# Order of the Gram and value products, and of the rounding steps of the hidden activations, in an attention and SwiGLU kernel

## The chip, the cores and the metric

The kernel runs on one core of one Trainium2 chip. The metric is the device time of one execution in microseconds (us); lower is better. Three runs of the kernel before took 283.43, 283.50 and 283.79 us, a median of 283.5.

## The reference

A polynomial-sketch attention is followed by a SwiGLU feed-forward block. `S1` and `S2` are 8 x 32 sketches.

```python
# q, k, v: (4 batches, 4 heads, 1088 tokens, 32)
def phi(x):                       # 64 features a token
    a = einsum('rd,bhsd->bhsr', S1, x); b = einsum('rd,bhsd->bhsr', S2, x)
    return einsum('bhsi,bhsj->bhsij', a, b).reshape(..., 64)
kv  = einsum('bhsf,bhsd->bhfd', phi(k), v);  z = phi(k).sum(2)
att = einsum('bhsf,bhfd->bhsd', phi(q), kv) / (einsum('bhsf,bhf->bhs', phi(q), z) + 1e-6)
x   = att, rearranged to (4352 tokens, 128)
g = x @ w_gate                    # 128 x 1536
out = (g * sigmoid(g) * (x @ w_val)) @ w_out    # w_out: 1536 x 128
```

The denominator needs only the sums of the key features. Since a feature is a product of two sketches, these sums are the 8 x 8 matrix of inner products of the two key sketches over the tokens: the "Gram" product of the code.

## The kernel before, in words

**Tokens and units.** The 4352 tokens are worked on transposed: 128 model dimensions on the partitions, tokens along the free axis. They are split into blocks: three of 384, 320 and 384 tokens for batch 0, then blocks of 480 and a last one of 384. The 1536 hidden columns are 12 chunks of 128. One block and one chunk make a *unit*: a gate product, a value product, a silu of the gate, a multiplication to the hidden activation `h`, and later a *down* product of `h` with `w_out` (`down`, L1024 or the cut form L1017, L1019, L1020).

**Cut products.** From the late units of the third block on, the gate and value products use operands that are cut into a rounded part, a remainder and a difference, so that they run in a shorter matmul format. For a unit, `start_unit` issues two products with the difference `xd` into a pair of PSUM banks (L937) and a scaling of that pair on ScalarE (L940). `finish_unit` issues four more products into the same banks (L949, L950), the silu on ScalarE (L952) and the multiplication on VectorE (L957). Three pairs of banks go around; the multiplication frees a unit's pair for the unit after the next two.

**The hidden activations.** For most chunks of the later blocks the down product is cut as well (the list `DOWN`). `cut_hidden` prepares three operands from `h`: the rounded `h1` (on ScalarE at L913, for some chunks on VectorE at L911), the remainder `h0 = h - h1` on GpSimd (L914), and `hd` on VectorE (L917), a difference of the scaled `h1` and `h`. It does not issue them at once. It puts them into two dictionaries by the number `y` of a unit: what is in `before` is issued inside `finish_unit(y)` ahead of the four products and the silu, what is in `behind` after the multiplication. The cut down product comes some five units later.

**Attention beside it.** Batch 0's attention is written out ahead. For batches 1 to 3 the generator `attentions` issues one step each time it is advanced (`parts_of`, `group`), between the units of the feed-forward block. A batch goes through: transposes of keys and queries, sketches of keys by matmul (`key_products`, L354) with copies on ScalarE (L566), features on VectorE (`key_features`, L377), the Gram product `gram` (L589) with a copy to SBUF on ScalarE (L595), the products of features and values `key_values` (L388), all into one bank, then `fold`: a small product (L601) that turns the Gram sums by the transposed sketch, and a multiplication on VectorE (L602) that leaves the denominators' weights in `s123`. `spread_out` turns and spreads the values' sums (L687 and six DMAs on SyncE) and loads the next batch's values. After that come the query sketches with `s123` (`query_sketches`, L342), the query features (`query_step`) and the numerators (L740), whose copies are the next tokens of the feed-forward block.

`turn_sketch` makes the transposed sketch once: a copy `four` on ScalarE (L578), a transposing product (L579) and a copy (L582).

**Order.** Nothing is scheduled by a tool: each engine runs its instructions in the order in which the program issues them, and waits on semaphores where data or buffers need it. So the order of the calls is the order of every engine's queue.

Of the kernel before, what the change touches and what calls it, by code (L numbers as in the profile page):

```python
# [12 lines left out]
AF = mybir.ActivationFunctionType  # L13
# [6 lines left out]
def kernel(  # L20
# [28 lines left out]
    nc = tc.nc  # L49
    P = nc.NUM_PARTITIONS  # L50
# [6 lines left out]
    NC = (NX + 3) // 4  # L57
    F = R * R
# [38 lines left out]
    def touch(*which):  # L97
        for i in which:
            clock[0] += 1
            used[i] = clock[0]  # L100
# [11 lines left out]
    def bank(tag=None):  # L112

        if tag is not None:
            i = place[tag]
        else:
            i = place[free_banks[turn[0] % len(free_banks)]]
            turn[0] += 1
        touch(i)
        return PS[:, i, :]  # L120

    def pair(keep=None):

        i = min((i for i in (0, 4, 6) if i not in held), key=lambda i: max(used[i], used[i + 1]))
        touch(i, i + 1)
        if keep is not None:
            held.add(i)
            kept[keep] = i
        return PS[:, i : i + 2, :]
# [3 lines left out]
    def let_go(keep):  # L133
        i = kept.pop(keep)
        held.discard(i)
        touch(i, i + 1)
# [26 lines left out]
    def load_k(b):  # L163
        nc.sync.dma_start(
            out=kld[:, 0:NX, :], in_=k[b].rearrange("h (pp x) d -> (h pp) x d", pp=32)
        )
# [158 lines left out]
    def turn_k(c0, c1):  # L325
        four = "p (a c) d -> p a c d"
        nc.vector.transpose(
            out=kT[:, c0:c1, :, :].rearrange("p c a t -> p a c t"),
            in_=kld[:].rearrange(four, a=4)[:, :, c0:c1, :],
        )  # L330
# [53 lines left out]
    def key_values(kv, phk, c0, c1, order=range(NC)):  # L384

        for c in range(c0, c1):
            for h in range(H):
                nc.tensor.matmul(  # L388
                    kv[32 * h : 32 * h + 32, 0:F],
                    vld[:, h, c, :],  # L390
                    phk[:, c, h, :, :].rearrange("p i j -> p (i j)"),
                    start=(c == order[0]),
                    stop=(c == order[-1]),
                )
# [148 lines left out]
    def turn_keys(b):  # L543

        for c in kpieces:
            turn_k(*c)
            if c[1] == NC and b + 1 < B:
                load_k(b + 1)
            yield
# [22 lines left out]

    sketch_turned = const.tile([P, P], FP32, name="s1t")

    def turn_sketch(ps):

        four = apool.tile([P, 4, H, R], FP32, tag="fold", name="four")
        nc.scalar.copy(four[:], s12[:, :, 0, :].unsqueeze(1).to_broadcast([P, 4, H, R]))  # L578
        nc.tensor.matmul(  # L579
            ps, four[:].rearrange("p a h r -> p (a h r)"), ident[:], start=True, stop=True  # L580
        )
        nc.scalar.copy(sketch_turned[:], ps)  # L582

    def gram(kv, kab):

        flat = "p x r -> p (x r)"
        for c in range(NC):
            x, a = slice(H * c, H * c + H), c % 4
            nc.tensor.matmul(  # L589
                kv[32 * a : 32 * a + 32, F : F + H * R],  # L590
                kab[:, 0, x, :].rearrange(flat), kab[:, 1, x, :].rearrange(flat),
                start=(c < 4), stop=(c >= NC - 4),
            )
        g = apool.tile([P, H * R], FP32, tag="gram", name="gram")
        nc.scalar.copy(g[:], kv[:, F : F + H * R])  # L595
        return g

    def fold(kv, g):

        ps = kv[:, 2 * F : 2 * F + H * R]  # L600
        nc.tensor.matmul(ps, sketch_turned[:], g[:], start=True, stop=True)  # L601
        nc.vector.tensor_tensor(  # L602
            out=s123[:, :, 2, :].rearrange("p (x h) r -> p x h r", x=2),
            in0=ps.rearrange("p (x h r) -> p x h r", x=1, r=R).to_broadcast([P, 2, H, R]),
            in1=own[:].unsqueeze(1).unsqueeze(3).to_broadcast([P, 2, H, R]),
            op=ALU.mult,
        )

    def attentions():

        yield from turn_keys(1)
        kp = pair("keys")
        turn_sketch(kp[:, 1, 320 : 320 + P])
        kab, copies = sketched(kp, key_products, 2, "kab2")
        run_copies(copies, 2)
        let_go("keys")
        yield from turn_queries(1)
        phk = apool.tile([P, NC, H, R, R], FP32, tag="phk", name="phk")  # L620
        yield from features(phk, kab)
        yield from turn_keys(2)
        kvz = pair("values")
        g = gram(kvz[:, 0, :], kab)
        key_values(kvz[:, 0, 0:F], phk, 0, NC)
        kab, copies = sketched(pair(), key_products, 2, "kab2")
        run_copies(copies, 2)
        fold(kvz[:, 0, :], g)
        spread = spread_out(1, kvz[:, 0, :])
        let_go("values")  # L630
        yield
        qab, copies = sketched(pair(), query_sketches, 3, "qab")
        run_copies(copies, 2)
        yield
        yield from query_step(1, qab)
        numerators(1, spread)
        yield "first"

        phk = apool.tile([P, NC, H, R, R], FP32, tag="phk", name="phk")
        yield from features(phk, kab)  # L640
        yield from turn_keys(3)
        yield from turn_queries(2)
        for b in (2, 3):
            yield "pe"
            if b == 3:
                numerators(2, spread)
            kv = bank("g2")
            g = gram(kv, kab)
            key_values(kv[:, 0:F], phk, 0, NC)
            if b == 2:  # L650
                kab, copies = sketched(pair(), key_products, 2, "kab2")
                run_copies(copies, 2)
            fold(kv, g)
            spread = spread_out(b, kv)
            yield
            yield "pe"
            qab, copies = sketched(pair(), query_sketches, 3, "qab")
            run_copies(copies, 2)
            yield
            if b == 2:  # L660
                yield from turn_queries(3)
                phk = feats[:].rearrange("p s (n h i j) -> p (s n) h i j", h=1, i=R, j=R)
                phk = phk.rearrange("p (c h) o i j -> p c (h o) i j", h=H)
                yield from features(phk, kab)
            yield from query_step(b, qab)
        yield "pe"
        numerators(3, spread)
        yield

    def run_copies(copies, n):  # L670
        for f, *args in copies[:n]:
            f(*args)
        del copies[:n]
# [102 lines left out]
    CUT = 1.0 - 2.0**-13  # L776
# [4 lines left out]
    def whole(ap):  # L781
        return ap.bitcast(FP32)
# [74 lines left out]
    before, behind = {}, {}  # L857

    def add_to(where, y, f):
        where.setdefault(y, []).append(f)  # L860
# [41 lines left out]
    def cut_hidden(y, i, j):  # L902

        if len(h_sets) < (5 if i < line[2] else OWN):
            h_sets.insert(0, next(h_rooms))
        n = SPLIT if i == LAST else blocks[i][1]
        h_sets.append(h_sets.pop(0))
        h1, h0, hd = h_parts[i, j] = [x[:, 0:n] for x in h_sets[-1]]
        h = hidden[i, j][:, 0:n]
        if j in ((2, 5, 8, 10) if i > line[2] else (9,)):  # L910
            add_to(before, y + 1, lambda: nc.vector.tensor_scalar(h1, h, CUT, None, op0=ALU.mult))  # L911
        else:
            add_to(behind, y + 1, lambda: nc.scalar.activation(h1, h, AF.Copy, scale=CUT))  # L913
        add_to(before, y + 2, lambda: nc.gpsimd.tensor_tensor(  # L914
            out=h0, in0=h, in1=whole(h1), op=ALU.subtract
        ))
        add_to(before, y + 3, lambda: nc.vector.scalar_tensor_tensor(  # L917
            out=hd, in0=whole(h1), scalar=WHOLE, in1=h, op0=ALU.mult, op1=ALU.subtract
        ))

# [196 lines left out]
    ps = bank("acc")  # L1117
# [23 lines left out]
    for t, c in zip(("acc", "g1", "g2"), (aside, c0, c1)):  # L1141
        ps = bank(t)
# [3 lines left out]
    n = steps[0][1]  # L1146
    pss = query_products(*steps[0], "ab")
    qbs = [query_copy(n, *ps) for ps in pss]
    phk = apool.tile([P, NC, H, R, R], FP32, tag="phk", name="phk")
# [10 lines left out]
    kvz = [apool.tile([P, P], FP32, name=x) for x in ("kvz0", "kvz1")]  # L1160
    nc.scalar.copy(zq[:], kz)
    kv = bank("acc")[:, 0:F]
# [7 lines left out]
    ps = bank("g0")  # L1170
# [8 lines left out]
    ps = bank("g1")  # L1179
# [16 lines left out]
    def parts_of(n):  # L1196

        for _ in range(n):
            if ahead[0] not in ("pe", "end"):
                ahead[0] = next(att, "end")  # L1200
# [96 lines left out]
    for n in range(ND):  # L1297
        if n == ND - 2:
            start_unit(2, 6)
        next_down()  # L1300
        parts_of(n in (0, 1, 7, 10, 11, 12))
        at(*steps_at.get(n, ()))
        if n == 9:
            catch_up(nc.vector)
# [58 lines left out]
    for y in range(END):  # L1363
# [16 lines left out]
        for k, c0, c1, tag, t0 in down_steps.get(y, ()):  # L1380
            if k == 0:
                n = c1 - c0
# [4 lines left out]
    ps = wide("a")[:, 0, 0:D]  # L1387
# [42 lines left out]
```

## Time and profile before

| quantity | value |
|---|---|
| median of three runs | 283.5 us |
| the profiled execution's own time | 283.42 us |
| its span | 281.7 us |
| granted TensorE clock, mean | 0.999 of full speed |
| TensorE matmul busy | 270.2 us, 96% of the span |
| VectorE busy | 221.1 us, 79% |
| ScalarE busy | 195.7 us, 69% |
| GpSimd busy | 98.7 us, 35% |
| waits of the value products (L388) for the copy of the Gram sums, in L388's own matmul row | 2.8 us, 3 times |

The profile is one execution, taken by the hardware's profiler. The span lies between its first and its last instruction; the execution's own time is some 1.7 us longer. PE is TensorE's matmul queue, PEld its weight loads, DVE is VectorE, ACT is ScalarE, POOL is GpSimd, SP is SyncE, which only issues DMAs here. A row of the timeline gives the start, the duration, the engine, the source line and operation, output and input, how often it runs in a row, and in brackets how long the engine was idle before it and which instruction ended that. A float32 matmul shows as two instructions. A row of the waits gives who waited for whom, the total in us, the number of times and the longest.

### The profile page before, as it was taken

To read this page: it belongs to the slowest core of one execution; us is meant where nothing else is said; L and a number is where in the kernel's file an instruction comes from. 1 tells how busy PE (TensorE), PEld (TensorE's weight loads), DVE (VectorE), ACT (ScalarE), POOL (GpSimd) and SP (SyncE) were. 2 spreads that over 40 slices of the span, in tenths; PEclk is the share of its full clock that TensorE was granted. 3 is DMA by queue.
4 is the path that set the end of the run, shared out by engine and by line. 5 is a ranking of instruction groups with operands and counts; after the bars stand their busy time and mean duration, and the time that the engine had idled before them with its cause. 6 is when DMAs were issued, how large, how long until landed. Compare 5 with 4: busy or idle time off the path is not lost.

```text
span 281.7 us, 5882 instructions
## 1 busy us (share of the span) xinstructions
PE 270.2 (96%) x2235; PEld 202.6 (72%) x2235; DVE 221.1 (79%) x376; ACT 195.7 (69%) x356; POOL 98.7 (35%) x110
## 2 busy tenths in 40 slices
PE   8899999997999989999999999799999999999995
PEld 7555566564895777767667878576888788789994
DVE  3997988798488762787627899976996996998871
ACT  3467665561586567777558999568888888887880
POOL 3315322064032010111016667433555553653430
PEclk9999999999999999999999999999999999999999
DMA  6584195222331041100200002000200200020021
GB/s 194 160 227 114 47 255 161 81 79 59 64 84 26 0 106 47 54 0 0 38 11 7 1 0 35 0 3 0 37 0 0 35 3 0 4 32 2 0 35 28
DMA packets 26139, 14.30 MB, mean 51 GB/s; under 512 B 19840, under 2 KB 24192, under 8 KB 26112
## 3 DMA queue, kind: packets, MB, share of 16 engines
q1 hardware_dynamic: 25456, 13.84, 19.8%
q8 instruction: 17, 0.28, 0.4%
q10 hardware_dynamic: 656, 0.10, 0.2%
q14 instruction: 10, 0.08, 0.1%
HBM read 11.41 MB, written 2.23 MB: 48 GB/s over the span
## 4 chain that ended last, share of the span: by engine, by line
PE 83%; DVE 9%; ACT 3%; issue 2%; DMA 1%; SPq 0%; DVEq 0%; ACTq 0%
PE PS L1024 15%; PE PS L937 13%; PE PS L949 13%; PE PS L950 13%; PE PS L973 10%; PE PS L1017 3%; PE PS L1019 3%; PE PS L1020 3%; PE PS L354 2%; PE PS L740 2%; PE PS L342 2%; PE PS L388 2%; DMA kld<-in_k_dram 1%; DVE phk L377 1%; DVE hbuf L957 1%
## 5 line engine op out<-in xcount | busy, mean ns | idle before, releaser
L940 ACT ACTIVATE PS<-PS 128x960 f32<-128x960 f32 (+1 forms) x90 | 83.3, 926 | 30.0 <-PE PS L937 29.0
L957 DVE SCALAR_TENSOR_TENSOR hbuf<-PS,sg 128x480 f32<-128x480 f32 (+1 forms) x87 | 55.0, 633 | 29.9 <-ACT sg L952 28.5
L952 ACT ACTIVATE sg<-PS 128x480 f32<-128x480 f32 (+1 forms) x90 | 49.6, 551 | 2.6 <-PE PS L950 2.2
L1024 PE MATMUL PS<-hbuf,wo 128*128 128x480 f32 (+3 forms) x122 | 50.7, 512 | 0.0
L937 PE MATMUL PS<-xd,graw 128*128 128x480 f32 (+1 forms) x69 | 36.0, 521 | 0.0
L937 PE MATMUL PS<-xd,wd 128*128 128x480 f32 (+1 forms) x90 | 34.0, 377 | 1.8 <-DVE hbuf L957 1.8
L949 PE MATMUL PS<-x,w 128*128 128x480 f32 (+1 forms) x90 | 33.4, 371 | 0.0
L950 PE MATMUL PS<-x,wb 128*128 128x480 f32 (+1 forms) x90 | 33.2, 369 | 0.0
L1024 PEld LDWEIGHTS PS<-hbuf,wo 128*128 128x128 f32 x122 | 22.8, 189 | 5.9 <-issue 0.4
L950 PE MATMUL PS<-x,graw 128*128 128x480 f32 (+1 forms) x69 | 25.5, 369 | 0.0
L937 PEld LDWEIGHTS PS<-xd,wd 128*128 128x128 f32 x90 | 17.0, 188 | 11.3 <-issue 4.5
L973 PE MATMUL PS<-xT,wg 128*128 128x384 f32 (+1 forms) x60 | 23.5, 474 | 0.1
L973 PE MATMUL PS<-xT,wv 128*128 128x384 f32 (+1 forms) x60 | 23.1, 467 | 0.3 <-DVE wv L286 0.3
L832 POOL TENSOR_TENSOR x<-xT,x 128x480 fp32r<-128x480 f32 (+1 forms) x6 | 7.2, 1195 | 40.7 <-ACT x L829 24.8
L914 POOL TENSOR_TENSOR hroom<-hbuf,hroom 128x480 fp32r<-128x480 f32 (+1 forms) x14 | 17.2, 1229 | 8.8 <-ACT hroom L913 4.3
L977 ACT ACTIVATE sg<-PS 128x384 f32<-128x384 f32 (+1 forms) x24 | 11.2, 468 | 13.0 <-PE PS L973 12.2
L949 PEld LDWEIGHTS PS<-x,w 128*128 128x128 f32 x90 | 16.9, 188 | 2.2
L950 PEld LDWEIGHTS PS<-x,wb 128*128 128x128 f32 x90 | 16.9, 188 | 2.1
L949 PE MATMUL PS<-x,graw 128*128 128x480 f32 (+1 forms) x48 | 18.0, 376 | 0.0
L937 PEld LDWEIGHTS PS<-xd,graw 128*128 128x128 f32 x69 | 13.0, 188 | 6.8 <-ACT PS L940 3.2
L973 PEld LDWEIGHTS PS<-xT,wv 128*128 128x128 f32 x60 | 11.2, 190 | 7.4 <-DVE hbuf L988 0.8
L973 PEld LDWEIGHTS PS<-xT,wg 128*128 128x128 f32 x60 | 10.9, 190 | 7.8 <-issue 1.1
(288 smaller groups left out, 567.6 us busy)
## 6 DMA issues: line engine op xcount, KB each, us to landing
kld<-in_k_dram SPq DMA_DIRECT2D x4, 544.0 KB, 4.0
vld<-in_v_dram SPq DMA_DIRECT2D x12, 144.0 KB, 4.8
qld<-in_q_dram SPq DMA_DIRECT2D x3, 544.0 KB, 4.0
raw<-in_moe_w_out_dram SPq DMA_DIRECT2D x4, 384.0 KB, 4.4
raw<-in_moe_w_gate_dram SPq DMA_DIRECT2D x3, 384.0 KB, 3.6
raw<-in_moe_w_val_dram SPq DMA_DIRECT2D x3, 384.0 KB, 3.7
out_dram<-o SPq DMA_DIRECT2D x16, 60.0 KB, 1.9
vld<-in_v_dram SPq DMA_DIRECT2D x4, 112.0 KB, 3.0
```

The source lines that it names most:

```text
L914: add_to(before, y + 2, lambda: nc.gpsimd.tensor_tensor(out=h0, in0=h, in1=whole(h1), op=ALU.subtract))
L937: nc.tensor.matmul(ps[:, k], w_parts[id(w), j // 3][2][:, j % 3, :], xd, start=True, stop=True)
L940: nc.scalar.activation(ps, ps, AF.Copy, scale=-1.0 / WHOLE)
L949: nc.tensor.matmul(ps[:, k], w1, x1, start=False, stop=False, skip_group_check=True)
L950: nc.tensor.matmul(ps[:, k], wb, x0, start=False, stop=True, skip_group_check=True)
L952: nc.scalar.activation(sg, ps[:, 0], AF.Silu, scale=WHOLE)
L957: nc.vector.scalar_tensor_tensor(out=hj[:, 0:n], in0=ps[:, 1], scalar=WHOLE, in1=sg, op0=ALU.mult, op1=ALU.mult)
L973: nc.tensor.matmul(o[:, 0:n], w[:, j, :], xT[:, t0 : t0 + n], start=True, stop=True)
L977: nc.scalar.activation(sg[:, 0:n], g[:, 0:n], AF.Silu)
L1017: nc.tensor.matmul(acc[i][:, 0:n], wd, hd, **sides)
L1019: nc.tensor.matmul(p, w1, h1, start=(j == mine[0]), stop=False)
L1024: nc.tensor.matmul(acc[i][:, 0:n], wo[:, j, :], hidden[i, j][:, 0:n], **sides)
```

## The change

It has three parts. (1) The copy `four` on ScalarE is issued at the start of `attentions`, two steps ahead of the product that reads it. (2) `key_values` is issued ahead of `gram`, and `fold` and `spread_out` come one step (one unit) later; for batch 1 this adds a step, and the list of units that advance the generator gets one more number, 8. (3) In `cut_hidden` the ScalarE rounding moves from behind the next unit's multiplication to ahead of its silu, the GpSimd subtraction from two units later to the next unit, and the VectorE difference from ahead of the multiplication three units later to behind the multiplication of the next unit. No instruction is added or removed on any engine. Lines behind the edits move by four to six numbers.

```diff
-    def turn_sketch(ps):
+    def four_sketches():
         four = apool.tile([P, 4, H, R], FP32, tag="fold", name="four")
         nc.scalar.copy(four[:], s12[:, :, 0, :].unsqueeze(1).to_broadcast([P, 4, H, R]))
+        return four
+
+    def turn_sketch(four, ps):
         nc.tensor.matmul(
...
+        four = four_sketches()
         yield from turn_keys(1)
         kp = pair("keys")
-        turn_sketch(kp[:, 1, 320 : 320 + P])
+        turn_sketch(four, kp[:, 1, 320 : 320 + P])
...
         kvz = pair("values")
+        key_values(kvz[:, 0, 0:F], phk, 0, NC)
         g = gram(kvz[:, 0, :], kab)
-        key_values(kvz[:, 0, 0:F], phk, 0, NC)
         kab, copies = sketched(pair(), key_products, 2, "kab2")
         run_copies(copies, 2)
+        yield
         fold(kvz[:, 0, :], g)
         spread = spread_out(1, kvz[:, 0, :])
...
             kv = bank("g2")
+            key_values(kv[:, 0:F], phk, 0, NC)
             g = gram(kv, kab)
-            key_values(kv[:, 0:F], phk, 0, NC)
             if b == 2:
                 kab, copies = sketched(pair(), key_products, 2, "kab2")
                 run_copies(copies, 2)
+            yield
             fold(kv, g)
             spread = spread_out(b, kv)
-            yield
             yield "pe"
...
         else:
-            add_to(behind, y + 1, lambda: nc.scalar.activation(h1, h, AF.Copy, scale=CUT))
-        add_to(before, y + 2, lambda: nc.gpsimd.tensor_tensor(
+            add_to(before, y + 1, lambda: nc.scalar.activation(h1, h, AF.Copy, scale=CUT))
+        add_to(before, y + 1, lambda: nc.gpsimd.tensor_tensor(
             out=h0, in0=h, in1=whole(h1), op=ALU.subtract
         ))
-        add_to(before, y + 3, lambda: nc.vector.scalar_tensor_tensor(
+        add_to(behind, y + 1, lambda: nc.vector.scalar_tensor_tensor(
             out=hd, in0=whole(h1), scalar=WHOLE, in1=h, op0=ALU.mult, op1=ALU.subtract
         ))
...
-        parts_of(n in (0, 1, 7, 10, 11, 12))
+        parts_of(n in (0, 1, 7, 8, 10, 11, 12))
```

## The prediction

> **What bounds the kernel now.** I read the shares by engine first, then the longest waits, then the timeline around each wait that stops TensorE.
>
> ```profile
> PE 270.2 (96%) x2235; PEld 202.6 (72%) x2235; DVE 221.1 (79%) x376; ACT 195.7 (69%) x356; POOL 98.7 (35%) x110
> PE 83%; DVE 9%; ACT 3%; issue 2%; DMA 1%; SPq 0%; DVEq 0%; ACTq 0%
> ```
>
> TensorE (PE) is busy for 96% of the 281.7 us span and carries 83% of the chain that ended last. A faster kernel can only come from the places where PE stands still. The waits name them:
>
> ```profile
> DVE hbuf L957 <- ACT sg L952: 28.5, 29, 3.2
> PE PS L388 <- ACT gram L595: 2.8, 3, 1.3
> PE PS L937 <- DVE hbuf L957: 1.8, 2, 1.1
> PEld PS L579 <- ACT four L578: 1.0, 1, 1.0
> ```
>
> The first line costs nothing by itself: VectorE (DVE) waits for ScalarE (ACT) while PE works. The other three stop PE, and the change touches all three. The timeline of PE shows them; the bracket is idle time before the instruction and who ended it:
>
> ```profile
> 52.09 0.81 PE L1024 MATMUL PS<-hbuf,wo 128*128 128x384 f32 x2
> 53.29 0.49 PE L579 MATMUL PS<-ident,four 128*128 128x128 f32 x2 [0.39 <-ACT four L578]
> ...
> 67.77 0.38 PE L589 MATMUL PS<-kab 128*32 128x32 f32 x18
> 69.41 1.21 PE L388 MATMUL PS<-phk,vld 128*32 128x64 f32 x72 [1.27 <-ACT gram L595]
> 70.55 1.27 PE L354 MATMUL PS<-s,kT 128*64 128x64 f32 x36
> ...
> 100.59 0.38 PE L589 MATMUL PS<-kab 128*32 128x32 f32 x18
> 101.88 1.21 PE L388 MATMUL PS<-phk,vld 128*32 128x64 f32 x72 [0.91 <-ACT gram L595]
> ...
> 141.40 0.38 PE L589 MATMUL PS<-kab 128*32 128x32 f32 x18
> 142.34 1.21 PE L388 MATMUL PS<-feats,vld 128*32 128x64 f32 x72 [0.57 <-ACT gram L595]
> ```
>
> The value products (L388) write another part of the bank that the copy of the Gram sums (L595) reads, and PE waits for that copy, which stands in ACT's queue behind other work. From 176 us on, the trouble is VectorE:
>
> ```profile
> 175.10 1.27 POOL L914 TENSOR_TENSOR hlate<-hbuf,hlate 128x480 fp32r<-128x480 f32 x1 [0.72 <-ACT hlate L913]
> 175.21 1.69 DVE L917 SCALAR_TENSOR_TENSOR hroom<-hroom,hbuf 128x480 fp32r<-128x480 f32 x1
> 176.81 0.65 DVE L957 SCALAR_TENSOR_TENSOR hbuf<-PS,sg 128x480 f32<-128x480 f32 x1
> 177.38 0.64 DVE L917 SCALAR_TENSOR_TENSOR hroom<-hroom,hbuf 128x480 fp32r<-128x480 f32 x1
> 177.51 0.49 PE L937 MATMUL PS<-xd,wd 128*128 128x480 f32 x1 [0.76 <-DVE hbuf L957]
> ```
>
> The same difference (L917) takes 0.64 us alone and 1.69 us when a GpSimd subtraction (L914) runs; it ends about 0.53 us after that one (176.37). PE waits for the multiplication (L957) queued behind it, since that frees the pair of banks. The second such stop is at 181.31 to 182.77.
>
> **Part 1, the copy `four`.** In the built order it moves on ACT from 52.95 to just ahead of the silu at 49.71, where ACT is idle for 1.39 us; that hides its 0.29 us (without the gap it would cost those). PE's pair of instructions at 52.09 takes 0.65 us by the chain, so it ends at 52.74 and L579 could start then instead of 53.29: 0.55 us. DVE was idle for 1.59 us before 56.57, waiting for the products behind this, so its queue moves up too. Bounds 0 and 0.55; I take 0.5, as nothing in the rows holds the products behind.
>
> **Part 2, values ahead of Gram, fold later.** The Gram product itself remains. Its 18 instructions, at the rate of L388 (72 in 70.55 − 69.41 = 1.14 us), are 0.29 us. So the three places give:
> - first: 1.64 − 0.29 = 1.35 us less a new wait. Working: L388, Gram, L354 (1.20 us) end at 67.77 + 2.63 = 70.40; three pairs of down products (0.27 us an instruction, 1.62) and the fold (0.24) bring PE to the query sketches (L342) at 72.26, before at 73.79. They read what the fold gives (L602). In the built order VectorE does the tokens' difference (L837, 0.56) ahead of it, and that waits for ACT: two key copies (0.69 from 70.5), then the rounding of tokens (0.53). So L602 ends near 72.5 and L342 starts near 72.6: gain 1.2. Bounds 0.6 (the fold's chain half a microsecond longer) and 1.5.
> - second: 101.88 − 100.59 − 0.29 = 1.0. VectorE's L602 now stands behind the multiplication of that unit (about 106.2), but L342 comes only near 107.
> - third: 142.34 − 141.40 − 0.29 = 0.65, covered the same way.
>
> Keys, queries, values and weights needed there are on chip (SP's order is unchanged). The six spreading DMAs and four value loads issue behind the fold, some 0 to 2 us later; their users come 14 us later or more (the values at 100.59, numerators at 88.52, 139.34, 188.63). The values' pair of banks is held one step longer; no paired unit starts in that time. Parts 1 and 2: 0.5 + 1.2 + 1.0 + 0.65 = 3.35 us.
>
> **Part 3, the rounding steps.** A unit takes PE 1.96 us when its down product is cut (158.29 to 160.25 between first products). 30 of the 46 roundings are on ACT (L913, 0.61 us; what follows starts 0.49 us later, 162.21 to 162.70). Ahead of the silu they delay it and the multiplication by 0.49 us. Slack: the multiplication at 201.61 ends at 202.26; the third-next unit's second product, which needs its bank, starts at 203.54, so 1.28 us become 0.79. New wait: the rounding waits for DVE's previous multiplication, and silu and the next bank scaling (L940) queue behind it. The circle silu to multiplication (160.40 − 159.79 = 0.61), multiplication 0.65, a hand-over of 0.08 (170.96 to 171.04, from ACT to GpSimd), rounding to silu 0.49 is 1.83 us, under 1.96: free while DVE is on time, but it catches up only 0.13 us a unit once late.
>
> What DVE gains: the subtraction starts when the rounding ends, the multiplication gives way 1.05 us later (0.61 from silu to multiplication, less 0.12 by which the silu starts before the rounding ends, and 0.57 to DVE's next instruction), the difference comes next, and the subtraction (1.23) is then nearly over: a wait of about 0.25 us instead of up to 1.05. From 160.40 to 182.07 VectorE is practically full; its differences there exceed 0.64 us by 1.0 + 0.46 + 1.05 + 1.04 = 3.55 us. Seven waits of 0.25 leave 1.75, so 1.8 is freed. Against it stand one more difference ahead of each multiplication (0.57) and the first delayed silu (0.49): net 0.7 off the two stops, which are 177.51 − 176.37 − 0.22 = 0.92 and 182.77 − 181.31 − 0.22 = 1.24, 2.16 us together. Bounds: 2.9 gained (both stops and the 0.7 before 190.83 vanish) and 2.5 lost (they double). I take 0.7, by the rows. In the wait for the last numerators (188.63 to 190.83) one more difference stands ahead of the releasing multiplication: 0.3 lost. From 196 us on no stop of PE is left to win, and 0.79 us of slack covers the delay: 0. The copies of sums and tokens on ACT keep their places.
>
> The Trainium skill, "SBUF — State Buffer", section "Who interferes with whom", has a rule that speaks against subtracting at once: a VectorE instruction with two SBUF inputs and a GpSimd one that reads SBUF exclude each other for a whole instruction, and issue order decides who blocks. The 1.69 against 0.64 us agrees with that. If by the rule every difference waited out a whole subtraction, the seven would pay 1.05 us each, 7.35 instead of 3.55, and the sum as an estimate would be a loss of 1.8 us, 285.2 us; by the starts in the rows they pay a quarter of it.
>
> Sum: 3.35 + 0.7 − 0.3 = 3.75 us; the profiled execution took 283.42 us, so 279.7 us. The median of the runs is 283.5, the same within 0.1.
>
> **Rivals.**
> - *All of VectorE's lateness goes* (differences never meet subtractions): 3.35 + 2.9 = 6.2, 277.2 us. For: the lengths alone and together. Against: the feature products (L377) still meet them. 0.13.
> - *The fold or another chain takes Part 2's place* (L342 waiting for L602; VectorE and GpSimd setting the pace at 56 to 66 us, where PE waits for `wo`): about 1.5 lost, 281.2 us. 0.12.
> - *VectorE's stops double*, since a late multiplication now holds the silu: 283.42 − 3.35 + 2.5 = 282.5 us. 0.08.
> - *Slower*: the circle through ACT becomes the bound. It does from the point where multiplications end more than 0.79 us late in most cut units; each rounding on ACT then costs PE time, and above 3.35/30 = 0.11 us each the gain is gone. At 0.15 us on 30 units: 283.42 − 3.35 + 4.5 = 284.6 us. Against: 1.83 is under 1.96. 0.09.
> - *Nothing moves*, PE's stops turning into others of the same size: 283.4 us. 0.03.
>
> **How the numbers follow.** The forecast has 0.55, with 278.6 to 280.9 as its own range. The range 277.2 to 282.5 leaves out the slower case, the unmoved one and about half of the two outer ones: about 0.2. Faster by over 0.2% (0.57 us, about what a measurement can tell): 0.55 + 0.13 + 0.12 + 0.08 = 0.88; same 0.03; slower 0.09.
>
> **What would show it.** Right: L388 starts within 0.1 us of the product ahead of it in all three places, and no wait of L388 for L595 or of L579 for L578 is listed; the mean of the 39 differences of 480 columns falls from 1.14 us (44.5 us in all) towards 0.9; PE's stops on L957 shrink. Wrong: a wait of L342 for L602 above 0.3 us; ACT idle ahead of L913, waiting for L957, in many units; PE stops on L937 after 196 us.

## The result: 280.1 us, and the profile after

The changed kernel takes 280.1 us (median of four runs, 279.65 to 280.17) against 283.64 us before (median of four runs); the ratio of the means is 0.986, 95% interval 0.983 to 0.990. A few executions take 1.4 to 2.1 us longer than the others of their kernel: one of these four of the kernel before (285.12 us), and below the profiled ones of two kernels in which GpSimd reads nothing (283.10 us beside a median of 281.02, 278.88 beside 277.43). Against the 283.5 us that the forecast starts from, the gain is 3.4 us. The forecast was 279.7 us. The profiled execution took 280.12 us with a span of 278.4 us, so 3.30 us less than the one before.

Behind the edits the lines have new numbers: L579 is now L583, L589 L593, L595 L599, L601 L605, L602 L606, L687 L693, L740 L746, L829 L835, L837 L843, L911 L917, L913 L919, L914 L920, L917 L923, L937 L943, L940 L946, L949 and L950 L955 and L956, L957 L963, L1024 L1030. L342, L354, L377 and L388 keep theirs.

The page's busy times and its chain by engine show TensorE's share up and VectorE's busy time down by 7.2 us, though VectorE executes as many instructions as before:

```profile
PE 270.4 (97%) x2235; PEld 202.9 (73%) x2235; DVE 213.9 (77%) x376; ACT 196.2 (70%) x356; POOL 102.4 (37%) x110
PE 88%; DVE 7%; ACT 2%; issue 2%; POOL 0%; DVEq 0%; ACTq 0%
```

In TensorE's own waits, those of L388 and L583 are gone. The multiplication still stops TensorE twice, for 1.5 us in sum after 1.8. They are not the same two stops: the first of before is gone, the second stands as it was (1.08 us idle, now at 178.75), and one came anew at 198.28:

```profile
PE PS L943 <- DVE hbuf L963: 1.5, 2, 1.1
```

TensorE's timeline at the places of Parts 1 and 2. L583 follows the down product directly, and L388 its predecessor without an idle bracket, in the first place and in the third:

```profile
52.20 0.81 PE L1030 MATMUL PS<-hbuf,wo 128*128 128x384 f32 x2
52.85 0.38 PE L583 MATMUL PS<-ident,four 128*128 128x128 f32 x2
...
66.59 0.70 PE L1030 MATMUL PS<-hbuf,wo 128*128 128x320 f32 x2
67.22 1.21 PE L388 MATMUL PS<-phk,vld 128*32 128x64 f32 x72
...
71.77 2.16 PE L342 MATMUL PS<-s,qT 128*32 128x96 f32 x72
73.86 0.44 PE L943 MATMUL PS<-xd,graw 128*128 128x384 f32 x1
...
137.61 1.20 PE L746 MATMUL PS<-phT,spread 32*32 32x288 f32 x34
138.74 1.21 PE L388 MATMUL PS<-feats,vld 128*32 128x64 f32 x72
```

Where the time went is read by setting the start of one and the same instruction in both profiles side by side. How much earlier it starts in the changed kernel:

| up to | before | after | earlier by | step | forecast |
|---|---|---|---|---|---|
| L579, now L583 | 53.29 | 52.85 | 0.44 | 0.44 (0.55 from the product ahead of it, 52.09 and 52.20) | 0.5 |
| first paired unit behind the first place | 75.41 | 73.86 | 1.55 | 1.1 | 1.2 |
| behind the second | 109.68 | 107.00 | 2.68 | 1.1 | 1.0 |
| behind the third | 149.88 | 146.32 | 3.56 | 0.9 | 0.65 |
| behind VectorE's two stops | 182.77 | 178.75 | 4.02 | +0.46 | +0.7 |
| behind the last numerators | 190.83 | 186.90 | 3.93 | −0.1 | −0.3 |
| behind 200 us | 216.80 | 213.59 | 3.21 | −0.7 | 0 |

Six steps stand near the forecast, within 0.25 us. The last one was not forecast: a new stop of TensorE. The timeline of VectorE, GpSimd and TensorE there:

```profile
193.82 0.36 DVE L917 TENSOR_SCALAR hroom<-hbuf 128x480 fp32r<-128x480 f32 x1
194.10 0.64 DVE L963 SCALAR_TENSOR_TENSOR hbuf<-PS,sg 128x480 f32<-128x480 f32 x1
194.32 1.23 POOL L920 TENSOR_TENSOR hroom<-hbuf,hroom 128x480 fp32r<-128x480 f32 x1 [1.54 <-DVE hroom L917]
194.67 1.39 DVE L923 SCALAR_TENSOR_TENSOR hroom<-hroom,hbuf 128x480 fp32r<-128x480 f32 x1
195.58 1.56 POOL L920 TENSOR_TENSOR hlate<-hbuf,hlate 128x480 fp32r<-128x480 f32 x1
195.99 1.67 DVE L843 SCALAR_TENSOR_TENSOR xd<-x,xT 128x480 fp32r<-128x480 f32 x1
197.58 0.65 DVE L963 SCALAR_TENSOR_TENSOR hbuf<-PS,sg 128x480 f32<-128x480 f32 x1
...
198.28 0.49 PE L943 MATMUL PS<-xd,wd 128*128 128x480 f32 x1 [0.42 <-DVE hbuf L963]
```

Read it from the top. VectorE rounds this chunk itself (L917), right ahead of the multiplication. That starts GpSimd's subtraction at 194.32, which runs to 195.55. The difference of the same chunk stands right behind the multiplication; it starts at 194.67, in the middle of the subtraction, and takes 1.39 us instead of 0.64. By then the next chunk's subtraction starts, and the token difference (L843) meets that one: 1.67 us. The next multiplication starts at 197.58, 3.48 us behind the last, and TensorE waits for the banks that it frees.

Over the whole kernel the differences tell which chunks this hits. I paired each rounding with its difference, in order. Of the 30 chunks rounded on ScalarE none takes over 1.3 us (mean of 0.77, the small blocks included); of the 16 rounded on VectorE, 13 take 1.30 us or more. Before, the long ones were spread over both kinds. The mean of the 39 of 480 columns is 1.02 us, where 1.14 was measured before and 0.9 expected.

### The profile page after: what moved, and what is told of

Same layout as the page of the kernel before. It is cut to its first block, busy times and chain, and to the rows that moved or that the text cites. A ratio compares the mean times of both kernels' runs of the same rounds, so it can differ in the third digit from the quotient of the medians.

```text
span 278.4 us, 5875 instructions
## 1 busy us (share of the span) xinstructions
PE 270.4 (97%) x2235; PEld 202.9 (73%) x2235; DVE 213.9 (77%) x376; ACT 196.2 (70%) x356; POOL 102.4 (37%) x110
## 4 chain that ended last, share of the span: by engine, by line
PE 88%; DVE 7%; ACT 2%; issue 2%; POOL 0%; DVEq 0%; ACTq 0%
PE PS L1030 17%; PE PS L943 14%; PE PS L955 13%; PE PS L956 13%; PE PS L979 10%; PE PS L1023 3%; PE PS L1025 3%; PE PS L1026 3%; PE PS L342 2%; PE PS L746 2%; PE PS L241 2%; PE PS L354 2%; PE PS L388 2%; DVE hbuf L963 1%; PE PS L1068 1%
## 5 line engine op out<-in xcount | busy, mean ns | idle before, releaser
L946 ACT ACTIVATE PS<-PS 128x960 f32<-128x960 f32 (+1 forms) x90 | 83.3, 926 | 26.6 <-PE PS L943 25.6
L963 DVE SCALAR_TENSOR_TENSOR hbuf<-PS,sg 128x480 f32<-128x480 f32 (+1 forms) x87 | 55.1, 634 | 39.9 <-ACT sg L958 33.1
L1030 PE MATMUL PS<-hbuf,wo 128*128 128x480 f32 (+3 forms) x122 | 50.7, 512 | 0.0
L943 PE MATMUL PS<-xd,graw 128*128 128x480 f32 (+1 forms) x69 | 35.8, 519 | 0.0
L943 PE MATMUL PS<-xd,wd 128*128 128x480 f32 (+1 forms) x90 | 34.1, 379 | 1.5 <-DVE hbuf L963 1.5
L955 PE MATMUL PS<-x,w 128*128 128x480 f32 (+1 forms) x90 | 33.4, 371 | 0.0
L956 PE MATMUL PS<-x,wb 128*128 128x480 f32 (+1 forms) x90 | 33.3, 370 | 0.0
L1030 PEld LDWEIGHTS PS<-hbuf,wo 128*128 128x128 f32 x122 | 22.8, 189 | 5.9 <-issue 0.4
L956 PE MATMUL PS<-x,graw 128*128 128x480 f32 (+1 forms) x69 | 25.5, 369 | 0.0
L943 PEld LDWEIGHTS PS<-xd,wd 128*128 128x128 f32 x90 | 16.9, 188 | 11.3 <-DVE hbuf L963 5.0
L920 POOL TENSOR_TENSOR hroom<-hbuf,hroom 128x480 fp32r<-128x480 f32 (+1 forms) x14 | 17.4, 1245 | 12.9 <-DVE hroom L917 5.2
L838 POOL TENSOR_TENSOR x<-xT,x 128x480 fp32r<-128x480 f32 (+1 forms) x6 | 8.3, 1390 | 28.8 <-ACT x L835 28.8
L955 PEld LDWEIGHTS PS<-x,w 128*128 128x128 f32 x90 | 16.9, 188 | 2.2
L956 PEld LDWEIGHTS PS<-x,wb 128*128 128x128 f32 x90 | 16.9, 188 | 2.1
L955 PE MATMUL PS<-x,graw 128*128 128x480 f32 (+1 forms) x48 | 17.9, 373 | 0.0
L943 PEld LDWEIGHTS PS<-xd,graw 128*128 128x128 f32 x69 | 13.0, 188 | 6.6 <-ACT PS L946 2.8
```

What stands on the lines that cost most here:

```text
L920: add_to(before, y + 1, lambda: nc.gpsimd.tensor_tensor(out=h0, in0=h, in1=whole(h1), op=ALU.subtract))
L943: nc.tensor.matmul(ps[:, k], w_parts[id(w), j // 3][2][:, j % 3, :], xd, start=True, stop=True)
L946: nc.scalar.activation(ps, ps, AF.Copy, scale=-1.0 / WHOLE)
L955: nc.tensor.matmul(ps[:, k], w1, x1, start=False, stop=False, skip_group_check=True)
L956: nc.tensor.matmul(ps[:, k], wb, x0, start=False, stop=True, skip_group_check=True)
L963: nc.vector.scalar_tensor_tensor(out=hj[:, 0:n], in0=ps[:, 1], scalar=WHOLE, in1=sg, op0=ALU.mult, op1=ALU.mult)
```

## The experiments

Each kernel ran beside the kernel before, whose median was 283.47 to 283.58 us every time.

| kernel | median, us | ratio to before | 95% interval | mean of the 39 differences, us |
|---|---|---|---|---|
| Parts 1 and 2 | 279.64 | 0.9865 | 0.9852 to 0.9878 | 1.14 |
| Part 3 alone | 283.96 | 1.0015 | 1.0006 to 1.0024 | 1.02 |
| changed, VectorE chunks' difference one unit later | 278.25 | 0.9815 | 0.9801 to 0.9828 | 0.80 |
| values ahead of Gram, fold as before | 280.74 | 0.9902 | 0.9887 to 0.9917 | 1.14 |
| changed, GpSimd reads nothing | 278.78 | 0.9836 | 0.9822 to 0.9851 | 0.75 |
| changed, rounding and subtraction as before | 281.33 | 0.9926 | 0.9913 to 0.9940 | 1.21 |
| Parts 1 and 2, differences behind, two units on | 279.79 | 0.9867 | 0.9854 to 0.9881 | 1.16 |
| Part 1 | 283.03 | 0.9979 | 0.9971 to 0.9988 | 1.14 |
| changed, all roundings on ScalarE | 278.28 | 0.9817 | 0.9803 to 0.9831 | 0.76 |
| before, GpSimd reads nothing | 281.02 | 0.9910 | 0.9896 to 0.9924 | 0.65 |
| changed, all on ScalarE, GpSimd reads nothing | 277.43 | 0.9793 | 0.9768 to 0.9817 | 0.75 |

### The parts by themselves

**Parts 1 and 2**: the diff of the change without its last piece in `cut_hidden`.

> Parts 1 and 2 alone, the rounding steps as in the kernel before. Theory: these two parts hold the whole gain (3.56 us by the starts of PE's rows in the two profiles), and Part 3 gave back about 0.3 us net, since its stop at 197 us is new; so this kernel takes 283.6 - 3.6 = 280.0 us or a little less, 279.7 to 280.1, and PE's two stops of 0.92 and 1.24 us at 176 and 181 us (before) are there again, without a stop of more than 0.3 us at 197 us. Rival (the forecast's sum): Part 3 is worth 0.4 us, and this kernel takes 280.5 us.

279.64 us. The stops of the kernel before are back, unchanged (1.8 us in two waits), and there is none at 197 us:

```profile
PE PS L943 <- DVE hbuf L963: 1.8, 2, 1.1
```

So these two parts hold the whole gain, 3.94 us by the medians.

**Part 3 alone**:

```diff
-            add_to(behind, y + 1, lambda: nc.scalar.activation(h1, h, AF.Copy, scale=CUT))
-        add_to(before, y + 2, lambda: nc.gpsimd.tensor_tensor(
+            add_to(before, y + 1, lambda: nc.scalar.activation(h1, h, AF.Copy, scale=CUT))
+        add_to(before, y + 1, lambda: nc.gpsimd.tensor_tensor(
...
-        add_to(before, y + 3, lambda: nc.vector.scalar_tensor_tensor(
+        add_to(behind, y + 1, lambda: nc.vector.scalar_tensor_tensor(
```

> Part 3 alone, on the kernel before. Theory: it moves stops of PE without removing any in sum: 283.6 to 284.0 us, with one stop before 183 us much smaller and a new one after 196 us. Rival (the forecast's sum): 0.4 us faster, 283.2 us. Second rival (the roundings on ScalarE hold the silu back in most units): over 284.5 us, with PE waiting for L957 and L940 in many units.

283.96 us, 0.38 us slower than the kernel before in the same rounds; the interval excludes no change. The forecast's 0.4 us of gain is refuted. The new stop is there too, at 201.07 to 202.26 us.

**Part 1 alone**: `four_sketches` is called early, nothing else changes.

> Part 1 alone, on the kernel before. Theory (the forecast's term, and the shift of 0.54 us between the profiles at 64 us): 283.05 us, 0.5 us faster. Rival: the gain is taken back at the next wait for the copy of the Gram sums, which stands in ScalarE's queue by the clock of other work and not by PE's: 283.4 us or more.

283.03 us, 0.55 us gained. Part 2 then holds 283.03 − 279.64 = 3.39 us.

**Values ahead of Gram without the later fold**:

```diff
-            g = gram(kv, kab)
             key_values(kv[:, 0:F], phk, 0, NC)
+            g = gram(kv, kab)
```

The same swap is made for batch 1 (`kvz`).

> The kernel before with key_values ahead of gram alone: the fold stays in the same step, nothing else is changed. Theory: the wait of L388 for the copy of the Gram sums goes, but the fold's small product, which also reads that copy, waits for it where no other product stands between (batch 3) and partly where the key products (1.2 us) do (batches 1 and 2): about two thirds of Part 2's gain, 281.5 us, with waits of L601 for L595 of 0.1 to 0.4 us twice and of about 1 us once. Rival: the order alone holds the gain, and the later fold is worth nothing: 280.5 us. Second rival: the wait only changes its place, 283.4 us.

280.74 us: 2.84 us gained, near the rival's 280.5 and not my two thirds. The order of the two products is most of Part 2; the later fold adds about 3.39 − 2.84 = 0.55 us. TensorE's timeline shows where. In batch 1 the key products (L354) cover the copy of the Gram sums, and the fold's product (L601) follows without a wait; in batch 2 it is the same. In batch 3 no product stands between:

```profile
68.95 0.35 PE L589 MATMUL PS<-kab 128*32 128x32 f32 x18
69.23 1.27 PE L354 MATMUL PS<-s,kT 128*64 128x64 f32 x36
70.43 0.41 PE L601 MATMUL PS<-gram,s1t 128*128 128x32 f32 x2
...
140.02 0.35 PE L589 MATMUL PS<-kab 128*32 128x32 f32 x18
140.66 0.41 PE L601 MATMUL PS<-gram,s1t 128*128 128x32 f32 x2 [0.29 <-ACT gram L595]
```

Against the kernel with Parts 1 and 2, L388 of batch 3 starts 0.52 us later here (138.99 and 138.47; Part 1 is missing), and the query sketches behind it 0.99 us later (145.42 and 144.43). The later fold earns its half microsecond in that one place.

### Why Part 3 loses

**The difference of the VectorE chunks one unit later**:

```diff
-        add_to(behind, y + 1, lambda: nc.vector.scalar_tensor_tensor(
+        add_to(behind, y + 2 if j in ((2, 5, 8, 10) if i > line[2] else (9,)) else y + 1,
+               lambda: nc.vector.scalar_tensor_tensor(
```

> The changed kernel, but for the chunks whose rounding is on VectorE the difference goes behind the multiplication one unit later (behind, y + 2). Theory: of these chunks the difference meets the GpSimd subtraction (1.39 to 1.41 us instead of 0.64 to 0.75), because their rounding is issued right ahead of the multiplication; one unit later the subtraction is over, the difference takes 0.65 us, the multiplication behind it comes in time, and the new stop of PE at 197 us (0.7 us) goes, perhaps that at 177 us (1.24 us) too: 279.4 us, down to 278.5. Rival: the lateness comes from the number of VectorE's instructions and not from the meeting: 280.1 us, with the stops where they were.

278.25 us, 0.25 below what was expected, and faster than the changed kernel by 1.85 us. No wait of L943 for L963 is left in TensorE's list. The same place as above, VectorE and GpSimd:

```profile
192.70 0.64 DVE L963 SCALAR_TENSOR_TENSOR hbuf<-PS,sg 128x480 f32<-128x480 f32 x1
192.92 1.22 POOL L920 TENSOR_TENSOR hroom<-hbuf,hroom 128x480 fp32r<-128x480 f32 x1 [1.54 <-DVE hroom L917]
193.26 1.39 DVE L843 SCALAR_TENSOR_TENSOR xd<-x,xT 128x480 fp32r<-128x480 f32 x1
194.58 0.66 DVE L963 SCALAR_TENSOR_TENSOR hbuf<-PS,sg 128x480 f32<-128x480 f32 x1
195.16 1.09 DVE L923 SCALAR_TENSOR_TENSOR hroom<-hroom,hbuf 128x480 fp32r<-128x480 f32 x1
```

One long instruction (the token difference) now stands between the two multiplications instead of two, and the next multiplication starts at 194.58, 1.88 us behind the last, instead of 3.48 us. Of the 16 differences of these chunks none takes over 1.3 us; of all 39 of 480 columns, one.

**All roundings on ScalarE**:

```diff
-        if j in ((2, 5, 8, 10) if i > line[2] else (9,)):
+        if j in ():
```

> The changed kernel with all 46 roundings on ScalarE (16 of them were on VectorE). Theory: only the chunks rounded on VectorE have differences that meet the subtraction; with all on ScalarE, nearly all differences take 0.65 to 0.75 us, PE's stops at 177 and 197 us go, and ScalarE carries it (rounding 0.51, silu 0.48, scaling 0.86 us from start to start, 1.85 us a unit under PE's 1.96): 278.2 to 278.8 us. Rival (the forecast's slower case): the circle through ScalarE becomes the bound where chunks with rounding follow each other; PE waits for L946 or L963 in many units: over 280 us.

278.28 us, the same gain by the other way: with no rounding on VectorE no difference takes over 1.3 us, and no wait of TensorE for the multiplication is listed any more. The edit also takes away the roundings that VectorE did beside a GpSimd subtraction: in the changed kernel two of the 16 took 1.42 and 1.22 us beside the subtraction for the tokens (L838), against 0.40 alone. So the run before this one isolates the differences, and this one does not. It also refutes the forecast's slower case: with all 46 roundings ahead of the silu, ScalarE (203.6 us busy) does not become the bound.

**Rounding and subtraction back in their old places, the difference at once**: L919 `behind, y + 1`, L920 `before, y + 2`, L923 as changed.

> The changed kernel, but with ScalarE's rounding and GpSimd's subtraction back in their old places (behind, y + 1; before, y + 2), the difference still behind the next unit's multiplication. Theory: the rounding then ends about when the multiplication ends, the subtraction and the difference start together in all chunks, every difference takes 1.4 us or more, and PE stops more than in the changed kernel: 281 to 283 us; it is the rounding ahead of the silu that keeps the difference of the ScalarE chunks clear of the subtraction. Rival: ScalarE's roundings ahead of the silu cost more (0.49 us of delay each) than the meetings: under 280 us.

281.33 us, as the theory had it, though not in all chunks: the mean difference is 1.21 us, with 33 of 39 over 0.9. The rounding ahead of the silu is needed where the difference follows the next multiplication.

**All differences behind the multiplication two units on, roundings as before**:

```diff
-        add_to(before, y + 3, lambda: nc.vector.scalar_tensor_tensor(
+        add_to(behind, y + 2, lambda: nc.vector.scalar_tensor_tensor(
```

> Parts 1 and 2, roundings and subtractions as in the kernel before, and all differences behind the multiplication two units on (behind, y + 2) where the kernel before had them ahead of the one three units on. Theory: the subtraction is over by then for chunks of both kinds, the differences take about 0.65 us, and the roundings need not stand ahead of the silu: 278.2 us, like the kernel with the late difference of the VectorE chunks. Rival: a rounding behind the multiplication starts the subtraction so late that it meets the other VectorE instructions with two operands (the next token difference, the feature products) as before: 279 to 279.6 us.

279.79 us, not 278.2, and no better than Parts 1 and 2 alone (279.64): my theory of this run fell, and the rival's reason came nearer, but not with the instructions that it named. VectorE and GpSimd show which meet:

```profile
174.82 0.65 DVE L963 SCALAR_TENSOR_TENSOR hbuf<-PS,sg 128x480 f32<-128x480 f32 x1
175.04 1.23 POOL L920 TENSOR_TENSOR hkld<-hbuf,hkld 128x480 fp32r<-128x480 f32 x1 [2.11 <-PE PS L956]
175.39 1.40 DVE L923 SCALAR_TENSOR_TENSOR hlate<-hlate,hbuf 128x480 fp32r<-128x480 f32 x1
```

The difference of one chunk (`hlate`) meets the subtraction of the *next* (`hkld`). A chunk's own subtraction being over is not enough. With a cut unit every 1.96 us and a subtraction of 1.23, some 0.73 us of each unit is free of subtractions, and a difference needs 0.64. It fitted where, in each unit, the subtraction starts ahead of the multiplication and a difference follows behind it: rounding, then multiplication beside the subtraction, then the difference, as the ScalarE chunks of the changed kernel have it. The difference need not be of the same chunk: with the VectorE chunks' difference one unit later it was not. That no other order would do is not shown.

### Is it the reading, and what else was there

**GpSimd reads nothing** in the place of this subtraction (its subtractions for the tokens and the weights stay), in the changed kernel and, with `y + 2`, in the kernel before:

```diff
-            add_to(before, y + 1, lambda: nc.gpsimd.tensor_tensor(
-                out=h0, in0=h, in1=whole(h1), op=ALU.subtract))
+            add_to(before, y + 1, lambda: nc.gpsimd.memset(whole(h0), 0.0))
```

> The kernel before with a constant written to the remainder h0 by GpSimd in the place of the subtraction (the remainder of h is left out of the down products). Theory (the forecast's reading of the two stops): PE's stops at 177.51 and 182.77 us (0.92 and 1.24 us) come from the meetings with the subtraction, and go: 281.4 us, the waits of L388 and L579 unchanged. Rival: VectorE is late there for the feature products and the transposes alone: 283.0 us or more.

281.02 us, 2.54 us less, and all 39 differences take 0.61 to 0.65 us. No wait of the product for the multiplication (L937 for L957 in the kernel before) is left. In the profiled execution (283.10 us) the same products start 2.11 us later than before at 75.41 us, where no instruction has changed yet. From there it makes up 0.91 us at the first stop (before, 177.51) and 1.24 at the second (182.77), just what the forecast read there. So the two stops of 2.16 us in sum, on which Part 3 was built, did come from the meetings; the forecast read them rightly.

> The changed kernel with a constant written to the remainder h0 by GpSimd in the place of the subtraction: GpSimd keeps its instructions, places and hand-overs, but reads nothing, and the remainder of h is left out of the down products. Theory: the long differences come from GpSimd's reading of two operands while VectorE reads two; without it all 39 differences of 480 columns take 0.64 to 0.66 us, PE's stops at 177 and 197 us go, and the time is that of the kernel with the late difference or less: 277.9 to 278.4 us. Rival: the differences are long because of what they write or where they stand in VectorE's queue: lengths and time stay, 280.1 us.

278.78 us, 0.4 above the range. The two stops went, but 5 of the 39 differences still take over 0.9 us (1.02 to 1.71). They are exactly the five that meet a subtraction that GpSimd still does, for the tokens (L838) or the weights (L881, L885); the other 34, of which five run beside writes alone, take 0.63 to 0.65. One of the five:

```profile
208.57 1.22 POOL L838 TENSOR_TENSOR x<-xT,x 128x480 fp32r<-128x480 f32 x1 [10.23 <-ACT x L835]
208.60 1.71 DVE L921 SCALAR_TENSOR_TENSOR hroom<-hroom,hbuf 128x480 fp32r<-128x480 f32 x1
```

So the reading makes the differences long, not their place in the queue. And a new stop had come: L941's second product starts 1.93 us behind the first, where 0.59 is usual behind a pair of down products, so 1.3 us are lost (I had counted 1.7, with the step of 0.22 that holds elsewhere). In the timeline, GpSimd's writes, the VectorE rounding among them and TensorE's row behind (the rounding is still L917; the multiplication is L961 here, the next products L941):

```profile
233.45 0.50 POOL L920 MEMSET hkld<- 128x480 f32 x1
233.88 0.50 POOL L920 MEMSET hqld<- 128x480 f32 x1
233.95 2.46 DVE L917 TENSOR_SCALAR hkld<-hbuf 128x480 fp32r<-128x480 f32 x1
...
235.21 0.94 POOL L920 MEMSET hroom<- 128x480 f32 x2
...
237.02 0.48 PE L941 MATMUL PS<-xd,wd 128*128 128x480 f32 x1 [1.18 <-DVE hbuf L961]
```

**Both edits**, to tell what made this stop:

> The changed kernel with both edits: all 46 roundings on ScalarE, and a constant written to the remainder h0 by GpSimd in the place of the subtraction (the remainder of h is left out of the down products). It tells what made PE's stop of 1.7 us at 235 us in the run without the reading, where a VectorE rounding took 2.46 us beside five GpSimd writes in a row. Theory: the rounding itself, one input and one output in SBUF, was held up by the writes; with no rounding on VectorE the stop goes, all meetings with the subtraction are gone too, and the time is that of all roundings on ScalarE, 278.0 to 278.4 us: the meetings that are left in that kernel cost PE nothing. Rival: the stop came from the token difference and the stores of that place: it stays, 278.8 us or more.

277.43 us. The stop is gone with VectorE's roundings, so the rounding that the writes held up had made it. But the median is 0.85 us below that of all roundings on ScalarE, where I expected none. The six runs go from 277.37 to 279.21 us and the two intervals overlap, so the medians alone do not settle it; the timelines do better. The profiled execution (278.88 us) is behind that of all roundings on ScalarE by 1.34 us already at the first paired unit, where the instructions are the same, and makes up 0.7 us from there (1.32 us behind at 141 us, 0.66 at 187), 0.5 of it between 172 and 175 us. With the subtraction, two differences of 1.10 and 0.93 us and a token difference of 1.06 stand ahead of the multiplication at 172.49, and TensorE's product starts at 173.19, 0.06 us behind its end; without it the same three take 0.65, 0.65 and 0.62 us. The meetings that are left with all roundings on ScalarE do cost TensorE some half a microsecond, too finely split for the list of waits.

## Why the prediction was right, and where its steps were not

- **Part 1, 0.5 us**: 0.55 by the medians. The row-by-row sum held, and ScalarE's idle time hid the copy (it runs at 48.33 us in the changed kernel, and 1.21 us stay idle behind it).
- **Part 2, 2.85 us**: 3.39 by the medians. The waits of L388 went in all three places, as read. In the first place the weight loads of L342 do stand idle for 0.44 us until VectorE's work behind the fold (L693) ends, above the 0.3 us that the forecast had named as a sign of being wrong; at 0.27 us a down product TensorE itself loses some 0.2 of that. L342 has a pause of its own besides (2.16 us there); it is not the edit's, since the kernel with Parts 1 and 2, of the same instructions up to there, has 1.72. The term that was too small is the third place, 0.65 us. From the start of the three attention groups to the feed-forward product behind them TensorE took 2.33 us before (141.40 to 143.73), 1.92 with the order alone (138.99 to 140.91) and 1.31 in the changed kernel (138.74 to 140.05), which gets the fold's product back in the next unit for some 0.2 us: 0.8 gained. My sum priced the listed wait only, and said nothing of the fold's own product, which stood alone behind the others and would wait for the copy if the order alone were changed.
- **Part 3, +0.4 us**: wrong in sign, −0.4 us alone (283.96 against 283.58) and −0.5 on top of the other parts (280.1 against 279.64). Two statements failed. "Seven waits of 0.25": the ScalarE chunks pay less as a rule (0.75 instead of 0.64 us), but the forecast gave the VectorE chunks the same price, and 13 of the 16 pay some 0.75 us each (1.39). The edit leaves their rounding ahead of the multiplication and brings the difference to right behind it, so the subtraction of 1.23 us cannot be over. And "from 196 us on no stop of PE is left to win, and 0.79 us of slack covers the delay: 0": the slack was worked out for ScalarE's delay, and covers that, as the run with all roundings on ScalarE shows; it does not cover 0.75 us of a difference and 1.0 us of a token difference between the same two multiplications. The second stop did not shrink for the same reason: the profile has a VectorE chunk there (174.82, 1.41 us) ahead of feature products of 1.99 us. Set against Parts 1 and 2 by the starts of the same products, the changed kernel loses 0.26 us between 74 and 172 us (partly within what two profiles differ by), wins 0.66 at the first stop and nothing at the second, and loses 0.7 at the new one: the sum of some −0.4 is close to that of the medians.
- **The total** came within 0.4 us because Parts 1 and 2 brought 0.6 us more than forecast and Part 3 some 0.8 us less. That closeness is luck: two errors of opposite sign cancelled. Of what the forecast named to tell it by, the waits of L388 and L579 went as said, but the mean of the differences, expected near 0.9, came out at 1.02, and a named sign of being wrong appeared: a stop of TensorE for the multiplication after 196 us (198.28). Both point to the wrong step. ScalarE waited for the multiplication ahead of a rounding (L919) 5 times of 30, 3.3 us in all.
- **The rule on shared reads** from the Trainium skill, "SBUF — State Buffer", "Who interferes with whom", speaks in the direction of what was seen: with GpSimd reading nothing, a difference takes 0.65 us in the kernel before, and 1.14 with the subtraction there. Its loss of 1.8 us was an estimate for all differences; in the changed kernel 13 of 16 VectorE chunks paid a good part of a subtraction, the ScalarE chunks 0.1 us as a rule and 0.5 at most.
- **Two profiles of one stream of instructions** can differ. The changed kernel and Parts 1 and 2, the same up to 141 us, are 0.28 us apart there; the profiled executions of 283.10 and 278.88 us were 2.11 and 1.34 us behind before the first paired unit, on unchanged instructions. Steps below 0.3 us in the table of starts are not settled by it; the medians are what settles the parts.

Both ways of keeping the VectorE chunks clear beat the changed kernel: 278.25 us with their difference one unit later, 278.28 us with all roundings on ScalarE.

## What to carry to other kernels

Where two engines' readings lengthen each other, as here, the place of an instruction has to be right against every neighbour's subtraction, not only its own: write down the free stretch in each period (here 1.96 − 1.23 = 0.73 us) and what event both hang on. Price an edit for each kind of item that it touches; here 30 items gained and 16 lost, and a mean over all hid it. Where a product waits for a copy, look at what else reads that copy: a plain swap of two products brought most of the gain, and the moved reader the rest.

## What the runs showed of the hardware beyond that

VectorE's rounding has one input and took 0.40 us alone. Beside GpSimd's writes, which read nothing, it took 2.46 us: it started with five writes running or queued (the last two end at 236.15) and ended at 236.41, when all were done. That was the longest of 16: at 210.23 the rounding stood among three such writes, came in ahead of the third, which took 0.76 us instead of 0.50, and ended after 0.70. What decides between the two is open. The differences, with two inputs, were not held up by such writes (five beside writes alone took 0.64 to 0.65). The Trainium skill, "SBUF — State Buffer", "Who interferes with whom", says that a VectorE `tensor_scalar` may take both ports and then exclude GpSimd for a whole instruction, in order of issue; here the wait went on over several GpSimd instructions that followed each other without a gap.
